# Attention results laid out in DRAM by depth, then head; one load for a block's rows and one for its spread

## The chip, the cores and the metric

The kernel runs on one core of a Trainium2 chip. The metric is the device time of one execution in microseconds (us). The kernel before took 1828.97 us, the median of three runs (1827.23 to 1829.23).

## The reference

It mixes a 32-head attention block and a mixture of 64 tiny experts with a sigmoid gate, over 2048 tokens of width 1024. The change lies in the attention branch: the softmax-weighted sums of the heads, their layout, and the product with `wo`.

```python
B, S, D = x.shape; H = 32; Dh = D // H              # 1, 2048, 1024; Dh = 32
q, k, v = split_heads(x @ wqkv)
p = softmax(einsum("bhqd,bhkd->bhqk", q, k) * Dh ** -0.5)
o = einsum("bhqk,bhkd->bhqd", p, v)
a = o.transpose(0, 2, 1, 3).reshape(B, S, D) @ wo
...
g = sigmoid((x * gate_w).sum(-1, keepdims=True))
return g * a + (1 - g) * b                          # b: the experts' branch
```

## The kernel before

Four stages follow each other. First come the projections of queries and keys and those of the values, which also prepare sums and differences of the blocks of `wo` for a seven-product (Strassen-like) multiplication. Then the attention loop runs over 32 heads of 16 key tiles each (613 to 1644 us). The last 187 us multiply the results by `wo`.

In the attention loop TensorE makes scores into a ring of PSUM banks, ScalarE turns them into exponentials `P`, TensorE multiplies these by the values into `o`. The sums over the keys are formed by VectorE (`acc`) and by GpSimd, which adds four of the 16 tiles of a head (three of the last head's) into a tile `accd` with accumulating DMAs. When a head is done, `finish` copies its unnormalised result to `osb` and stores it to the DRAM tensor `od`. Its sums go to `smd` (`norm_sums`). After each fourth head, `load_r` loads the sums of the four heads of the group as `rr`, and `norm_r` takes the reciprocals, multiplies them by the gate, and stores them to `rd`.

The last stage works on eight blocks of W = 256 tokens. A block n needs two tiles of 128 x 8 x 256 numbers: `OC[n]`, the results of all heads (`load_o`, tile name `V`), and `RB[n]`, the reciprocals, spread over the 32 rows of each head (`load_rb`, tile name `rb` for block 0, else `accd`). Their second index is a group of four heads; there are G = KC = 8 groups. Blocks 0 and 1 go through plain products in fp32r, with high and low parts (`split_hi`, `split_lo`, `split_o`, `wo_mm`); here kc counts the groups, and `z` and `acc` are the high and low part of the results, `woh` and `wol` those of `wo`. The last group of block 0 can only be normalised once the last head's sums have come back from DRAM, so `wo_mm(pa, 0, [KC - 1], ...)` stands last. Blocks 2 to 7 are units of seven products (`unit`): `scale_o` normalises a block in place, `ht.operand` makes the sums S1 to S4 and their parts, and `ht.product` runs a product into one of eight PSUM banks in turn. The other factors of these products come from DRAM by `load_t` (`t0h` to `t3l`).

All orders are written out by hand. Each engine runs its instructions in program order. SyncE (SP in the profile) issues most DMAs, also in order, so a DMA that waits holds up those behind it. Semaphores of eight DMA slots are used in turn, so that a DMA also waits until the eighth before it has landed. Of the tiles `V` and of the tiles `accd` two exist at a time: the load of block n + 2 waits until block n has been used. In the attention loop, `at(step, f, ...)` hangs a call on a key tile.

```python
        if kc == 1:
            norm_sums(H - 1, sm, nc.scalar)
            load_r(G - 1)
...
    for (i, half), ps in pa.items():
        av_mm(0, i, half, ps)
    split_o(0, KC - 1, KC)
    wo_mm(pa, 0, [KC - 1], False, True)
```

Of the kernel before, what the change touches and what calls it, by code (L numbers as in the profile page):

```python
# [9 lines left out]
F32 = mybir.dt.float32  # L10
F32R = mybir.dt.float32r
# [20 lines left out]
def gated_mha_peer_kernel(ctx, tc, xT, wqkv, wv, wo, wq, k12, ug, v, out):  # L32
# [8 lines left out]
    nc = tc.nc  # L41
# [4 lines left out]
    dram = ctx.enter_context(tc.tile_pool(name="dram", bufs=1, space=bass.MemoryType.DRAM))  # L46
# [4 lines left out]
    VD = [dram.tile([S, 512], F32, name=f"vd{i}") for i in range(2)]  # L51
    WPD = dram.tile([128, KC, 512], F32, name="wpd")
    ATD = dram.tile([128, S], F32R, name="atd")
    OD = [dram.tile([128, S], F32, name=f"od{g}") for g in range(G)]
    ZD = dram.tile([1, S], F32, name="zd")
    SMD = [dram.tile([4, S], F32, name=f"smd{g}") for g in range(G)]
    RD = dram.tile([G, 4, S], F32, name="rd")

    TD = [[dram.tile([128, KC // 2, 512], F32R, name=f"t{i}{part}") for part in "hl"] for i in range(4)]
    VPD = [dram.tile([128, D], F32R, name=f"vp{part}") for part in "hl"]  # L60
# [13 lines left out]
    def dma(dst, src, queue=nc.sync):  # L74
        a, b = (ap.bitcast(F32) if ap.dtype == F32R else ap for ap in (dst, src))
        return queue.dma_start(a, b)  # L76
# [16 lines left out]
    def split(hi, lo, src, on=None):  # L93
        nc.scalar.activation(hi, src, AF.Copy)  # L94
        (on or nc.vector).tensor_tensor(out=lo, in0=src, in1=hi.bitcast(F32), op=OP.subtract)
# [805 lines left out]
    zp = Pool("zp", side="right")  # L901
# [210 lines left out]
    early = more[:, KC * W:].rearrange("p (a m) -> p a m", m=512)  # L1112
# [265 lines left out]
    def finish(h):  # L1378
        g, j = divmod(h, 4)
        o = wk.tile([128, 512], F32, name="osb")  # L1380
        nc.scalar.activation(o, O.pop(h), AF.Copy)
        dma(OD[g][32 * j:32 * j + 32, :].rearrange("d (q s) -> q d s", q=NQ), o)


    def norm_sums(h, ps, queue=nc.sync):
# [7 lines left out]
    def load_r(g):  # L1393
        R[g] = wk.tile([128, 128], F32, name="rr", bufs=1)[:, :64]
        dma(R[g], SMD[g].rearrange("j (b m) -> (j b) m", m=64))

    def norm_r(g):
        r = R.pop(g)
        nc.vector.reciprocal(r, r)
        nc.vector.tensor_mul(r, r, G64)  # L1400
        dma(RD[g].rearrange("j (b m) -> (j b) m", m=64), r)


    OC, RB = {}, {}

    def load_o(n, k0, k1, queue=nc.sync):
        if k0 == 0:
            OC[n] = vpool.tile([128, KC, W], F32, name="V")
        for kc in range(k0, k1):
            dma(OC[n][:, kc, :], OD[kc][:, n * W:(n + 1) * W], queue)  # L1410

    def load_rb(n, k0, k1, js=range(4), queue=nc.sync):
        if k0 == 0 and js[0] == 0:
            RB[n] = rb0 if n == 0 else wk.tile([128, KC, W], F32, name="accd")
        for j in js:
            src = RD[k0:k1, j:j + 1, n * W:(n + 1) * W].rearrange("g j s -> j g s")
            dma(RB[n][32 * j:32 * j + 32, k0:k1, :], src.to_broadcast([32, k1 - k0, W]), queue)

    def load_chunk(n, k0, k1, queue=nc.sync):
        load_o(n, k0, k1, queue)  # L1420
# [4 lines left out]
    OH, OL, W0 = {}, {}, []  # L1425
# [38 lines left out]
    at((H - 1) * NT + 13, merge, H - 1)  # L1464
    for k in range(2 * KC):
        c = slice(k % 2 * D // 2, (k % 2 + 1) * D // 2)
        at((8 + k) * NT + 11, dma, raw_wo(k // 2)[:, c], wo[:, k // 2 * D:(k // 2 + 1) * D][:, c])
    for i in range(2):
        at(28 * NT + 6 + i, dma, vhl[:, i], VPD[i])
    at(29 * NT + 13, load_o, 0, 0, 4)  # L1470
    at(30 * NT + 7, load_o, 0, 4, KC - 1)
    at(30 * NT + 13, load_rb, 0, 0, KC - 1, range(2))
    at((H - 1) * NT + 2, load_rb, 0, 0, KC - 1, range(2, 4))
    at((H - 1) * NT + 8, load_rb, 1, 0, KC - 1)
    at((H - 1) * NT + 14, load_rb, 2, 0, KC - 1)
# [113 lines left out]
    def split_o(n, k0, k1):  # L1589
        o = OC[n][:, k0:k1, :]  # L1590
        nc.vector.tensor_mul(o, o, RB[n][:, k0:k1, :])
# [8 lines left out]
    finish(H - 1)  # L1600
    sm = pso.tile([128, 512], F32, name="o")
    list(rowsum(sm, *(P[H - 1, NT - i] for i in (1, 2)), ACC.pop(H - 1)))
    load_o(1, 0, KC - 1, nc.gpsimd)
    split_hi(1)
    for kc in range(1, KC - 1):
        split_hi(kc + 1)
        if kc == 1:
            norm_sums(H - 1, sm, nc.scalar)
            load_r(G - 1)
            for n in range(2):  # L1610
                load_at(n)
# [12 lines left out]
    load_t(2, None, [fin.tile([128, S], F32R, name="t3l")])  # L1624
    load_t(0, *([keep.tile([128, S], F32R, name=f"wo_raw{j}")] for j in range(2)))
# [5 lines left out]
    OH[1] = zp.tile([128, KC, W], F32R, name="z1")  # L1631
    OL[1] = wk.tile([128, KC, W], F32R, name="acc")
# [138 lines left out]
```

## Time and profile before

| what | value |
| --- | --- |
| time, median of three runs | 1828.97 us |
| the profiled execution's own time | 1832.25 us |
| its span, from the first to the last instruction | 1830.4 us |
| mean granted TensorE clock | 0.999 |
| TensorE busy | 1817.8 us (99%) |
| VectorE busy | 1461.4 us (80%) |
| ScalarE busy | 1312.5 us (72%) |
| moved by DMA | 345.24 MB |

All times in rows of the profile are microseconds from the start of the span. A row of the timeline names start, duration, engine, line, operation and tiles; `xN` is the number of merged instructions, and a bracket at its end gives the time for which the engine sat idle before it and what released it. SPq and ACTq are the queues on which SyncE and ScalarE issue DMAs. A row of stages gives the stretch, its length, the busy time and count of each engine (PE is TensorE, PEld its weight loads, DVE VectorE, ACT ScalarE, POOL GpSimd), the granted clock, the busy share of the 16 DMA engines and GB/s. A matmul's row lasts longer than the distance to the next one's start, because matmuls are pipelined.

### The profile page before, as it was taken

The page shows a single profiled execution, that of the slowest core. Times are in us where ns is not written, and L with a number is a line of the kernel's source. Part 1 is how long each engine was busy: PE and PEld are TensorE (multiplying, and loading weights), DVE is VectorE, ACT ScalarE, POOL GpSimd, SP SyncE. Part 2 cuts the span into 40 slices and gives each one's busy share as a digit, 9 for nine tenths or more (in the row PEclk, how much of TensorE's full clock was granted, in tenths as well). Part 3 has the DMA queues.
Part 4 walks back from the last instruction along what each step waited for, and adds up shares of the span by engine and source line. Part 5 has one row for each costly group of instructions (what it writes and reads, how often), then busy time and mean ns, then how long its engine had stood idle before and what let it go on. Part 6 is the DMA issues. An engine that isn't in the chain of part 4 may idle for free.

```text
span 1830.4 us, 26559 instructions
## 1 busy us (share of the span) xinstructions
PE 1817.8 (99%) x10083; PEld 1099.8 (60%) x10083; DVE 1461.4 (80%) x1258; ACT 1312.5 (72%) x1716; POOL 231.7 (13%) x358
## 2 busy tenths in 40 slices
PE   9999999999999999999999999999999999999999
PEld 6777777788888644444444444444444444447787
DVE  7866876789967888888888888888888888884675
ACT  5545544522433699999999999999999999992221
POOL 1222222244001100000000000000000000010000
PEclk9999999999999999999999999999999999999999
DMA  7888689660267777776777777777777777776872
GB/s 271 277 277 280 209 296 286 199 215 9 83 240 247 219 157 178 158 177 154 177 176 164 186 165 182 171 173 167 174 186 159 178 159 182 174 138 180 281 164 78
DMA packets 127441, 345.24 MB, mean 189 GB/s; under 512 B 17168, under 2 KB 57904, under 8 KB 107920
## 3 DMA queue, kind: packets, MB, share of 16 engines
q1 hardware_dynamic: 95688, 193.40, 36.0%
q0 software_dynamic: 28224, 145.92, 34.1%
q10 hardware_dynamic: 3400, 4.20, 1.0%
q8 instruction: 80, 1.31, 0.3%
q14 instruction: 49, 0.40, 0.1%
HBM read 171.76 MB, written 72.36 MB: 133 GB/s over the span
## 4 chain that ended last, share of the span: by engine, by line
PE 88%; DMA 5%; issue 3%; DVE 1%; ACT 1%; SPq 1%; POOL 1%; DVEq 0%; ACTq 0%; POOLq 0%
PE ring L1317 28%; PE o L1338 25%; PE bk L302 15%; PE pa L963 5%; PE bk L724 5%; PE bk L982 2%; PE bk L290 2%; PE bk L341 2%; PE ring L1351 1%; PE bk L963 1%; SPq L76 1%; DMA accd<-rd 1%; DMA accd<-P 1%; DMA smd<-ssb 1%; DMA z<-t2h 1%
## 5 line engine op out<-in xcount | busy, mean ns | idle before, releaser
L1327 ACT ACTIVATE P<-ring 128x1024 f32<-128x1024 f32 (+2 forms) x1031 | 912.7, 983 | 14.5 <-DMA accd<-P 1.9
L1367 DVE TENSOR_TENSOR acc<-acc,P 128x2048 f32<-128x2048 f32 x319 | 730.9, 2291 | 72.6 <-ACT P L1327 47.1
L1338 PE MATMUL o<-P,V 128*32 128x512 f32 x3840 | 464.8, 599 | 0.0
L1317 PE MATMUL ring<-Q,K 98*128 98x512 f32 x1024 | 272.2, 407 | 0.4 <-ACT P L1327 0.3
L1317 PE MATMUL ring<-z,z 98*128 98x512 f32 x1020 | 270.6, 407 | 0.6 <-ACT accd L1327 0.6
L1317 PEld LDWEIGHTS ring<-Q,K 98*128 98x128 f32 x1024 | 182.0, 188 | 144.8 <-ACT P L1327 73.8
L1317 PEld LDWEIGHTS ring<-z,z 98*128 98x128 f32 x1020 | 181.3, 188 | 142.8 <-ACT P L1327 72.0
L1338 PEld LDWEIGHTS o<-P,V 128*32 128x32 f32 x3840 | 98.8, 109 | 223.1 <-issue 214.5
L1360 POOL DMA_DIRECT2D accd<-P x95 | 81.5, 858 | 931.5 <-ACT P L1327 406.5
L1365 DVE TENSOR_TENSOR acc<-P,P 128x2048 f32<-128x2048 f32 x32 | 73.4, 2293 | 74.8 <-ACT P L1327 74.8
L302 PE MATMUL bk<-xh,A 128*128 128x512 f32 x336 | 82.8, 396 | 0.0
L302 PE MATMUL bk<-xh,S 128*128 128x512 f32 x336 | 81.3, 393 | 0.0
L302 PE MATMUL bk<-xl,S 128*128 128x512 f32 x336 | 80.1, 391 | 0.0
L135 ACT ACTIVATE hi<-u 128x512 fp32r<-128x512 f32 x42 | 26.5, 632 | 70.0 <-issue 39.4
L302 PEld LDWEIGHTS bk<-xh,A 128*128 128x128 f32 x336 | 62.1, 188 | 23.8 <-issue 5.0
L1370 DVE TENSOR_TENSOR acc<-acc,accd 128x2048 f32<-128x2048 f32 x32 | 73.1, 2284 | 0.0
L302 PEld LDWEIGHTS bk<-xl,S 128*128 128x128 f32 x336 | 62.8, 188 | 16.3 <-issue 2.5
L302 PEld LDWEIGHTS bk<-xh,S 128*128 128x128 f32 x336 | 62.4, 188 | 14.5 <-issue 1.7
L1327 ACT ACTIVATE accd<-ring 128x1024 f32<-128x1024 f32 (+2 forms) x64 | 62.2, 1032 | 2.3 <-PE ring L1317 2.2
L963 PE MATMUL pa<-woh,acc 128*128 128x512 f32 x192 | 62.2, 389 | 0.0
L511 DVE TENSOR_TENSOR u<-u,bk 128x512 f32<-128x512 f32 x70 | 46.6, 682 | 10.0 <-DMA wpd<-u 5.8
L94 ACT ACTIVATE acc<-V 128x512 fp32r<-128x512 f32 x24 | 14.5, 625 | 50.8 <-DVE V L1576 14.4
(302 smaller groups left out, 2204.9 us busy)
## 6 DMA issues: line engine op xcount, KB each, us to landing
accd<-P POOLq DMA_DIRECT2D x95, 1024.0 KB, 7.6
wqt<-in_wq SPq DMA_DIRECT2D x64, 512.0 KB
wraw<-in_wqkv SPq DMA_DIRECT2D x28, 512.0 KB
kdh<-hi POOLq DMA_DIRECT2D x32, 256.0 KB, 5.3
kdl<-lo POOLq DMA_DIRECT2D x32, 256.0 KB, 6.5
qdh<-hi POOLq DMA_DIRECT2D x32, 256.0 KB, 5.9
qdl<-lo POOLq DMA_DIRECT2D x32, 256.0 KB, 5.9
z<-kdh SPq DMA_DIRECT2D x32, 256.0 KB
```

The source lines that it names most:

```text
L290: nc.tensor.matmul(b0[w, n], AW[PLAIN[w, ki]][a][:, k, :], X[f"B{ki + 1}{n + 1}"][b][:, k, :], start=first, stop=last)
L302: nc.tensor.matmul(ps, a[i][:, k, :], b[j][:, k, :], start=(k == 0 and i == j == 0), stop=(k == HC - 1 and i == 1))
L511: nc.vector.tensor_tensor(out=out, in0=a, in1=b, op=OP.add)
L724: nc.tensor.matmul(ps, x_part(a, t // 4, kc)[:, tok], b, start=first, stop=last)
L963: nc.tensor.matmul(ps, self.a[a][i][:, k, :], self.b[b][j][k], start=(not first and k == 0 and i == j == 0), stop=(k == HC - 1 and i == 1))
L1317: on_ring(nc.tensor.matmul(ring[:, i, :], K[:98, kt * 128:(kt + 1) * 128], Q[:98, qc * 512:(qc + 1) * 512], start=True, stop=True), i)
L1327: on_ring(nc.scalar.activation(P[h, kt][:, q0 * 512:(q0 + m) * 512].rearrange("p (a m) -> p a m", a=m), ring[:, i:i + m, :], AF.Exp, scale ...
L1338: nc.tensor.matmul(O[h][32 * qc:32 * qc + 32, :], Vt[g][:, kt, 32 * j:32 * j + 32], p[:, qc * 512:(qc + 1) * 512], start=(kt == 0), stop=( ...
L1360: nc.gpsimd.dma_start(ACCD[h], P[h, kt], accum_op=OP.add)
L1365: nc.vector.tensor_add(ACC[h], P[h, 0], P[h, kt])
L1367: nc.vector.tensor_add(ACC[h], ACC[h], P[h, kt])
L1370: nc.vector.tensor_add(ACC[h], ACC[h], ACCD[h])
```

## The change

The eight tensors `od0` to `od7` become one, ordered by quarter of the tokens, depth, head in its group, half, group and token. Row p of a block's tile is then 4 * depth + head instead of 32 * head + depth, and the 8 x 256 numbers of a row lie together in DRAM. `rd` is laid out likewise by head, block and group. So `load_o` becomes one DMA with up to 8 KB in a piece where it was one for each group with pieces of 1 KB, and `load_rb` becomes one DMA where it was four. The stores of `finish` now come in pieces of 1 KB where they were 2 KB. The rows of `wo` are loaded in the new order of rows. TensorE's instructions and their order stay the same. Several loads and steps move.

```diff
-    OD = [dram.tile([128, S], F32, name=f"od{g}") for g in range(G)]
+    OD = dram.tile([NQ, 32, 4, 2, KC, W], F32, name="od")
+    wo_rows = wo.rearrange("(j d) m -> d j m", j=4)
...
-    RD = dram.tile([G, 4, S], F32, name="rd")
+    RD = dram.tile([4, S // W, KC, W], F32, name="rd")
...
-            dma(early[:, j], wo[:, c0:c0 + 512])
+            dma(early[:, j], wo_rows[:, :, c0:c0 + 512])
...
-        dma(OD[g][32 * j:32 * j + 32, :].rearrange("d (q s) -> q d s", q=NQ), o)
+        dma(OD[:, :, j, :, g, :].rearrange("q d n s -> (q d) n s"),
+            o.rearrange("p (n s) -> p n s", n=2))
...
-        dma(RD[g].rearrange("j (b m) -> (j b) m", m=64), r)
+        dma(RD[:, :, g, :].rearrange("j n (q m) -> (j n) q m", m=64), r)
...
-        for kc in range(k0, k1):
-            dma(OC[n][:, kc, :], OD[kc][:, n * W:(n + 1) * W], queue)
+        dma(OC[n][:, k0:k1, :], OD[n // 2, :, :, n % 2, k0:k1, :].rearrange("d j g s -> (d j) g s"), queue)
...
-        for j in js:
-            src = RD[k0:k1, j:j + 1, n * W:(n + 1) * W].rearrange("g j s -> j g s")
-            dma(RB[n][32 * j:32 * j + 32, k0:k1, :], src.to_broadcast([32, k1 - k0, W]), queue)
+        src = RD[:, n, k0:k1, :].rearrange("j g s -> j (g s)")[None]
+        dma(RB[n][:, k0:k1, :].rearrange("p g s -> p (g s)"),
+            src.to_broadcast([32, 4, (k1 - k0) * W]), queue)
...
-    at(30 * NT + 13, load_rb, 0, 0, KC - 1, range(2))
-    at((H - 1) * NT + 2, load_rb, 0, 0, KC - 1, range(2, 4))
+    at(30 * NT + 13, load_rb, 0, 0, KC - 1)
     at((H - 1) * NT + 8, load_rb, 1, 0, KC - 1)
-    at((H - 1) * NT + 14, load_rb, 2, 0, KC - 1)
...
-    load_o(1, 0, KC - 1, nc.gpsimd)
     split_hi(1)
     for kc in range(1, KC - 1):
         split_hi(kc + 1)
...
                 load_at(n)
+            load_o(1, 0, KC - 1)
             pso.close()
         split_lo(kc)
         wo_mm(pa, 0, [kc], False, False)
-    norm_r(G - 1)
+        if kc == HC:
+            norm_r(G - 1)
     for n in range(2):
         load_chunk(n, KC - 1, KC)
-    load_rb(2, KC - 1, KC)
+    load_rb(2, 0, KC)
...
+    split_o(1, 0, HC)
+    split_o(0, KC - 1, KC)
+    load_o(2, 0, KC)
     load_t(0, *([keep.tile([128, S], F32R, name=f"wo_raw{j}")] for j in range(2)))
...
-    split_o(0, KC - 1, KC)
     wo_mm(pa, 0, [KC - 1], False, True)
-    for k0, k1 in ((0, HC), (HC, KC)):
-        split_o(1, k0, k1)
-    load_o(2, 0, KC)
+    split_o(1, HC, KC)
     load_at(2)
     load_t(2, [zp.tile([128, S], F32R, name="z0")], None)
     load_t(1, *([keep.tile([128, S], F32R, name=f"wo_raw{2 + j}")] for j in range(2)))
+    load_rb(3, 0, KC)
+    load_o(3, 0, KC)
     pa1 = banks4()
...
-    load_rb(3, 0, KC, queue=nc.scalar)
-    load_o(3, 0, KC)
```

The first place is SyncE's queue at the end of the attention loop. Before, from the loads of the reciprocals of blocks 1 and 2 (two tiles `accd`) to the loads of the last group (`od7`; the first `V` is block 0's, the other block 1's):

```order
L76 DMA accd_12321<-rd_88 32x7x256 x4
L76 DMA accd_12402<-rd_88 32x7x256 x4
L76 DMA od7_78<-osb_12457 4x32x512
L76 DMA rr_12490<-smd7_87 128x64
L76 DMA at_12492<-atd_70 128x256
L76 DMA at_12494<-atd_70 128x256
L76 DMA rd_88<-rr_12490 128x64
L76 DMA V_11936<-od7_78 128x256
```

The same place now:

```order
L77 DMA accd_12306<-rd_81 128x1x1792
L77 DMA od_71<-osb_12434 128x2x256
L77 DMA rr_12459<-smd7_80 128x64
L77 DMA at_12461<-atd_70 128x256
L77 DMA at_12463<-atd_70 128x256
L77 DMA V_12465<-od_71 128x1792
L77 DMA rd_81<-rr_12459 32x4x64
L77 DMA V_11929<-od_71 128x256
```

One DMA stands where eight stood ahead of the last head's store. Block 2's reciprocals are gone from here. Block 1's results (`V_12465`), which GpSimd issued in seven DMAs before, stand between the load of the sums and the store of the reciprocals.

The second place is VectorE in block 0, where the last group's sums are turned into reciprocals. Before, from group 4's parts (`wol4`) to those of block 1:

```order
L1553 TENSOR_TENSOR wol4_12435<-wo_raw1_5501,woh4_12428 128x1024
L1556 TENSOR_TENSOR acc_12286<-V_11936,z0_12285 128x256
L1549 TENSOR_TENSOR V_11936<-V_11936,rb0_5505 128x256
L1553 TENSOR_TENSOR wol5_12436<-wo_raw2_5502,woh5_12429 128x1024
L1556 TENSOR_TENSOR acc_12286<-V_11936,z0_12285 128x256
L1553 TENSOR_TENSOR wol6_12437<-wo_raw2_5502,woh6_12430 128x1024
L1556 TENSOR_TENSOR acc_12286<-V_11936,z0_12285 128x256
L1399 RECIPROCAL rr_12490<-rr_12490 128x64
L1400 TENSOR_TENSOR rr_12490<-rr_12490,G64_102 128x64
L1553 TENSOR_TENSOR wol7_12438<-wo_raw3_5503,woh7_12431 128x1024
L95 TENSOR_TENSOR wol0_12440<-wo_raw3_5503,woh0_12439 128x1024
L1591 TENSOR_TENSOR V_11936<-V_11936,rb0_5505 128x256
```

The same place now; block 1's tile is `V_12465`, block 0's `V_11929`:

```order
L1552 TENSOR_TENSOR wol4_12412<-wo_raw1_5494,woh4_12405 128x1024
L1555 TENSOR_TENSOR acc_12271<-V_11929,z0_12270 128x256
L1401 RECIPROCAL rr_12459<-rr_12459 128x64
L1402 TENSOR_TENSOR rr_12459<-rr_12459,G64_95 128x64
L1548 TENSOR_TENSOR V_11929<-V_11929,rb0_5498 128x256
L1552 TENSOR_TENSOR wol5_12413<-wo_raw2_5495,woh5_12406 128x1024
L1555 TENSOR_TENSOR acc_12271<-V_11929,z0_12270 128x256
L1552 TENSOR_TENSOR wol6_12414<-wo_raw2_5495,woh6_12407 128x1024
L1555 TENSOR_TENSOR acc_12271<-V_11929,z0_12270 128x256
L1552 TENSOR_TENSOR wol7_12415<-wo_raw3_5496,woh7_12408 128x1024
L96 TENSOR_TENSOR wol0_12417<-wo_raw3_5496,woh0_12416 128x1024
L1590 TENSOR_TENSOR V_12465<-V_12465,accd_12306 128x1024
```

The reciprocal moved ahead of five operations on groups 5 and 6, and the first half of block 1 moved ahead of the last group of block 0.

The third place is SyncE's queue behind that. Before, from the last of the eight DMAs for block 2's results (`V_12654`) to the loads of `t3h` into `woh`, behind which block 3's results stood (its reciprocals were on ScalarE's queue):

```order
L76 DMA V_12654<-od7_78 128x256
L76 DMA at_12663<-atd_70 128x256
L76 DMA z0_12665<-t2h_93 128x2048
L76 DMA wo_raw2_12667<-t1h_91 128x2048
L76 DMA wo_raw3_12668<-t1l_92 128x2048
L76 DMA out_0<-rb0_5505 128x512 x4
L76 DMA woh0_12439<-t3h_95 128x512
```

The same place now, from block 2's reciprocals (`accd_12572`) on:

```order
L77 DMA accd_12572<-rd_81 128x1x2048
L77 DMA t3l_12577<-t2l_87 128x2048
L77 DMA V_12587<-od_71 128x2048
L77 DMA wo_raw0_12589<-t0h_82 128x2048
L77 DMA wo_raw1_12590<-t0l_83 128x2048
L77 DMA at_12619<-atd_70 128x256
L77 DMA z0_12621<-t2h_86 128x2048
L77 DMA wo_raw2_12623<-t1h_84 128x2048
L77 DMA wo_raw3_12624<-t1l_85 128x2048
L77 DMA accd_12627<-rd_81 128x1x2048
L77 DMA V_12629<-od_71 128x2048
L77 DMA out_0<-rb0_5498 128x512 x4
```

Block 2's results (`V_12587`) stand ahead of `t0h` instead of behind `t0l`, and block 3's loads (`accd_12627`, `V_12629`) ahead of the stores of block 0.

More of the change, by code (lines that the diff above doesn't have):

```diff
@@ L1408, in load_o, with load_rb @@
             OC[n] = vpool.tile([128, KC, W], F32, name="V")
-        for kc in range(k0, k1):
-            dma(OC[n][:, kc, :], OD[kc][:, n * W:(n + 1) * W], queue)
-    def load_rb(n, k0, k1, js=range(4), queue=nc.sync):
-        if k0 == 0 and js[0] == 0:
+        dma(OC[n][:, k0:k1, :], OD[n // 2, :, :, n % 2, k0:k1, :].rearrange("d j g s -> (d j) g s"), queue)
+    def load_rb(n, k0, k1, queue=nc.sync):
+        if k0 == 0:
             RB[n] = rb0 if n == 0 else wk.tile([128, KC, W], F32, name="accd")
-        for j in js:
-            src = RD[k0:k1, j:j + 1, n * W:(n + 1) * W].rearrange("g j s -> j g s")
-            dma(RB[n][32 * j:32 * j + 32, k0:k1, :], src.to_broadcast([32, k1 - k0, W]), queue)
+        src = RD[:, n, k0:k1, :].rearrange("j g s -> j (g s)")[None]
+        dma(RB[n][:, k0:k1, :].rearrange("p g s -> p (g s)"),
+            src.to_broadcast([32, 4, (k1 - k0) * W]), queue)
     def load_chunk(n, k0, k1, queue=nc.sync):
@@ L1466, in gated_mha_peer_kernel @@
         c = slice(k % 2 * D // 2, (k % 2 + 1) * D // 2)
-        at((8 + k) * NT + 11, dma, raw_wo(k // 2)[:, c], wo[:, k // 2 * D:(k // 2 + 1) * D][:, c])
+        at((8 + k) * NT + 11, dma, raw_wo(k // 2)[:, c], wo_rows[:, :, k // 2 * D:(k // 2 + 1) * D][:, :, c])
     for i in range(2):
@@ L1624, in gated_mha_peer_kernel @@
     load_t(2, None, [fin.tile([128, S], F32R, name="t3l")])
+    OH[1] = zp.tile([128, KC, W], F32R, name="z1")
+    OL[1] = wk.tile([128, KC, W], F32R, name="acc")
+    split_o(1, 0, HC)
+    split_o(0, KC - 1, KC)
+    load_o(2, 0, KC)
     load_t(0, *([keep.tile([128, S], F32R, name=f"wo_raw{j}")] for j in range(2)))
@@ L1628, in gated_mha_peer_kernel @@
         av_mm(0, i, half, ps)
-    split_o(0, KC - 1, KC)
     wo_mm(pa, 0, [KC - 1], False, True)
-    OH[1] = zp.tile([128, KC, W], F32R, name="z1")
-    OL[1] = wk.tile([128, KC, W], F32R, name="acc")
-    for k0, k1 in ((0, HC), (HC, KC)):
-        split_o(1, k0, k1)
-    load_o(2, 0, KC)
+    split_o(1, HC, KC)
     load_at(2)
```

## The prediction

> **What bounds the kernel now.** The page's first part comes first.
>
> ```profile
> PE 1817.8 (99%) x10083; PEld 1099.8 (60%) x10083; DVE 1461.4 (80%) x1258; ACT 1312.5 (72%) x1716; POOL 231.7 (13%) x358
> L1327 ACT ACTIVATE P<-ring 128x1024 f32<-128x1024 f32 (+2 forms) x1031 | 912.7, 983 | 14.5 <-DMA accd<-P 1.9
> ```
>
> TensorE is the bound and leaves only 12.6 us. The second row shows the attention loop's exponentials, which run almost without a gap: the change touches neither these nor TensorE's work. What it can win lies in the last stage. There TensorE's timeline has three stalls, and the chain of waits gives the pace without one:
>
> ```profile
> 1661.38 1.07 PE L1522 MATMUL pa<-wol,z 128*128 128x512 f32 x4
> 1665.91 1.97 PE L1529 MATMUL pa<-vhl,at 128*128 128x512 f32 x8
> 1669.27 0.96 PE L1522 MATMUL pa<-woh,z 128*128 128x512 f32 x3 [1.39 <-ACT z L94]
> ...
> 1698.21 0.39 PE L963 MATMUL pa<-woh,acc 128*128 128x512 f32 x1
> 1699.36 0.47 PE L963 MATMUL pa<-z,s 128*128 128x512 f32 x1 [0.76 <-ACT osb L1678]
> ...
> 1720.08 0.39 PE L963 MATMUL pa<-woh,acc 128*128 128x512 f32 x1
> 1722.73 0.67 PE L963 MATMUL pa<-z,s 128*128 128x512 f32 x1 [2.26 <-DVE rb L969]
> 1727.15 1.08 PE L963 MATMUL pa<-wo_raw,s 128*128 128x512 f32 x4
> ...
> 1740.03 13.60 PE pa L963 x60
> 1760.88 13.60 PE pa L963 x60
> ```
>
> 60 matmuls in 13.60 us are 0.227 for one. By starts, the stalls cost: 1669.27 - 1665.91 - 8 x 0.227 = 1.55 us; 1699.36 - 1698.21 - 0.227 = 0.92; 1722.73 - 1720.08 - 0.227 = 2.42. Behind the third, a product's 12 matmuls took 1727.15 - 1722.73 = 4.42 us instead of 2.72: 1.70 more, at a clock of 0.60 (third number from the right in these rows of stages):
>
> ```profile
> 1722.80:1727.10 4.30, 4.30 (x12) 3.43 (x13) 3.52 (x7) 1.15 (x2) 0.00 (x0) 0.60 0.73 87
> 1750.00:1826.20 76.20, 76.16 (x336) 62.74 (x335) 49.53 (x75) 14.73 (x25) 0.00 (x0) 1.00 0.48 129
> ```
>
> From 1750 us on TensorE never waits. All there is to win in this stage is 1.55 + 0.92 + 2.42 + 1.70 = 6.59 us.
>
> **First stall: the last group's reciprocals.** The chain of waits and the timeline:
>
> ```profile
> 1650.21 10.26 DMA smd<-ssb
> 1660.54 0.34 SPq L76 DMA_DIRECT2D rr<-smd  x1
> 1662.86 0.55 DVE L1399 RECIPROCAL rr<-rr 128x64 f32<-128x64 f32 x1 [3.67 <-DMA rr<-smd]
> 1663.70 0.32 SPq L76 DMA_DIRECT2D rd<-rr  x1
> 1665.18 1.72 SPq L76 DMA_DIRECT2D rb<-rd  x4
> 1668.34 0.43 DVE L1591 TENSOR_TENSOR V<-V,rb 128x256 f32<-128x256 f32 x1 [2.40 <-DMA rb<-rd]
> 1668.80 0.42 ACT L94 ACTIVATE z<-V 128x256 fp32r<-128x256 f32 x1 [10.20 <-DVE V L1591]
> ...
> 1631.86 15.13 SPq L76 DMA_DIRECT2D accd<-rd  x8
> 1647.10 1.83 SPq L76 DMA_DIRECT2D od<-osb  x1
> V<-od POOLq DMA_DIRECT2D x7, 128.0 KB, 11.5
> 1650.00:1658.00 8.00, 8.00 (x37) 6.59 (x36) 6.46 (x12) 6.72 (x11) 0.00 (x0) 1.00 0.67 172
> ```
>
> The tiny store of the sums takes 10.26 us while the store `rd` took 1665.18 - 1663.70 = 1.48. In flight beside it are block 1's `V` from GpSimd (seven times 128 KB, landing 11.5 us after issue), block 2's `accd`, issued last of the eight, and the store `od`; the DMA engines are 0.67 busy. The change takes block 2's `accd` out, moves `V` behind the sums, and lets `od` go when its copy is done. So I price the sums like `rd`: issue 1.06 us on ScalarE's queue, then 1.16 (1.48 less its 0.32 of issue), plus 2.32 for loading `rr`: it lands at 1650.21 + 1.06 + 1.16 + 2.32 = 1654.8 us. The other end is 1662.9, as now.
>
> The added wait is the reciprocal's on VectorE, now ahead of groups 5 and 6:
>
> ```profile
> 1655.83 0.42 DVE L1549 TENSOR_TENSOR V<-V,rb 128x256 f32<-128x256 f32 x1
> 1656.17 1.22 DVE L1553 TENSOR_TENSOR wol<-wo_raw,woh 128x1024 fp32r<-128x1024 f32 x1
> 1658.78 0.42 DVE L1556 TENSOR_TENSOR acc<-V,z 128x256 fp32r<-128x256 f32 x1
> 1669.59 1.22 DVE L1591 TENSOR_TENSOR V<-V,accd 128x1024 f32<-128x1024 f32 x1
> 1670.85 1.06 ACT L94 ACTIVATE z<-V 128x1024 fp32r<-128x1024 f32 x1 [1.63 <-DVE V L1591]
> ```
>
> VectorE reaches it at 1655.8, after the sums land, so it waits for nothing. From there, with 1.22 for the low part of half a block too: 0.84 (1662.86 to the issue of `rd` at 1663.70), 3.37 (1655.83 to 1659.20), two `wol` 2.44, half of block 1 now ahead of the last group 1.22 + 1.06 + 1.22, then 0.46 + 0.47 until TensorE has `z`: 11.1 us, 1666.9. TensorE wants it at 1665.91 + 8 x 0.227 = 1667.7. The stall of 1.55 goes, with 0.8 to spare; sums that land after 1656.6 bring it back.
>
> Block 1's load, 0.9 MB, stands ahead of the store `rd`: 917 KB at the 422 GB/s shown below is 2.2 us, done by about 1657, when `rd` is issued. Hidden by groups 5 and 6.
>
> **Second and third stall: loads in SyncE's queue.**
>
> ```profile
> 1672.59 15.92 SPq L76 DMA_DIRECT2D V<-od  x8
> 1689.23 9.99 DMA z<-t2h
> 1707.50 4.78 SPq L76 DMA_DIRECT2D V<-od  x8
> 1713.45 1.23 DVE L1576 TENSOR_TENSOR V<-V,accd 128x1024 f32<-128x1024 f32 x1 [3.99 <-DMA V<-od]
> ...
> 1632.00:1636.00 4.00, 4.00 (x27) 1.95 (x25) 3.90 (x3) 4.00 (x5) 0.00 (x0) 1.00 1.12 219
> 1674.00:1678.00 4.00, 4.00 (x19) 3.34 (x18) 2.72 (x4) 2.03 (x3) 0.00 (x0) 1.00 1.01 422
> ```
>
> Eight DMAs for block 2 held SyncE for 15.92 us, so `t2h` was issued at 1689.23 and landed at 1699.22: that, not ScalarE, ended the second stall. Now one DMA loads block 2's results instead of eight, and pieces of 8 KB move at 422 GB/s (the `t0` loads) where those of 1 KB move at 219. Block 2's load waits for VectorE's last use of block 0, about 1667.5. Behind it follow `t0h`, `t0l` and `t2h`, four times 1.05 MB: 10 us, landing near 1680, 17 us before it is wanted. 0.92 us gone.
>
> In the third stall VectorE waited 3.99 us for block 3's results, issued at 1707.50, and so released the product's bank late. The new place needs block 1's tiles free (about 1671); with what stands ahead it is the last of 8.5 MB from 1667.5 on: 20 us, landing near 1688, while VectorE asks at 1709.5. Freed of 3.99 us, it releases the bank 1.6 us before TensorE wants it. 2.42 us and, with the clock drop, 1.70 go. The next to be late would be `t3h`, issued behind block 0's stores near 1690 and wanted in unit 2's last product, over 20 us later.
>
> [...]
>
> **The loop.** Block 0's reciprocals come in one load in head 30:
>
> ```profile
> 1598.41 1.03 SPq L76 DMA_DIRECT2D rb<-rd  x2
> 1599.79 10.48 DMA accd<-P
> 1610.35 1.94 ACT L1327 ACTIVATE P<-ring 128x512 f32<-128x512 f32 x2 [0.93 <-DMA accd<-P]
> 1611.00 0.50 PE L1317 MATMUL ring<-Q,K 98*128 98x512 f32 x1 [0.31 <-ACT P L1327]
> ```
>
> The slow accumulation (10.48 us) starts amid these loads of 458 KB into 64 rows. Now 917 KB go in large pieces. Ends: ScalarE's 0.93 won, or as much lost again; I take TensorE's 0.31 as won, the loads being the shorter at 422 GB/s. Stores of `od` in 1 KB pieces have 32 us each; the loads of `wo` have the same sizes: nothing.
>
> **The sum.** 6.59 + 0.31 = 6.90 us. The profiled execution took 1832.25 us (span 1830.4), 3.28 above the median; it would take 1825.35. The median, 1828.97, becomes 1822.1.
>
> **Rivals.** 0.2%, 3.7 us, is about what can be told from no change.
>
> - The first stall stays (sums land at 1657 to 1659, or block 1 ahead of the last group costs more): 1822.1 + 1.55 = 1823.6. The mere 0.8 us to spare speak for it. 0.14.
> - The slow stretch stays, its cause another than the wait: 1822.1 + 1.70 = 1823.8. Against it: in the 76 us without a stall the clock is 1.00. [...] 0.04.
> - The sums land at 1662.9 as now. VectorE is held 7.0 us; `wol` of group 5 comes at 1662.9 + 0.84 + 0.34 + 1.22 = 1665.3 where TensorE wants it at 1661.4: 3.9, then 2.4 for the last group, and 1.7 of slow clock. 8.0 - 1.55 = 6.45 lost against 5.35 won: 1830.1, no change. 0.12.
> - The third stall isn't the load's but ScalarE's and VectorE's own pace: won 1.55 + 0.92 + 0.31 only, 1826.2. Against it: units 4 to 7 run without a stall. 0.07.
> - Slower: spreading 8 KB from one place to 32 rows is slow. Place: `accd` of blocks 4 to 7. TensorE's unit lasts 20.9 us (1740.03 to 1760.88 in the chain), its DMAs 0.48 of it, 10 us, of which 1 MB at 219 GB/s, 4.8, is this load. It decides once the load takes over 15.7 us, below 67 GB/s. At a quarter of 219 it takes 19.2: 3.5 late in each of four units, 14 less 6.9: 1836.1. Against it: the same numbers are spread 32 times now. 0.13.
>
> **Chances and range.** The forecast has 0.50. Faster: 0.50 + 0.14 + 0.04 = 0.68; same: 0.12 + 0.07 = 0.19; slower 0.13. The range runs from 1820.4 (0.6 more from the loop, 1.1 of spread between runs) to 1830.6 (late sums and 0.5 of spread), leaving out the slow spread and little else.
>
> **What would show it.** `rr` on VectorE starting before 1657 us counted from a loop that ends at 1643.8; no wait of TensorE over 0.3 us between 1644 and 1826; clock 1.00 there; no wait for `V<-od` on VectorE in units 2 and 3. A reciprocal that waits, a slow stretch without a wait, or `accd<-rd` ending waits in units 3 to 6 would prove the rivals.

## The result, and the profile after

The changed kernel takes 1825.84 us, the median of 11 executions (1824.19 to 1826.57). The kernel before takes 1829.84 us, the median of 11 on the same chip (1827.23 to 1833.42). The ratio is 0.9977, with an interval of 0.9967 to 0.9986: some 4.2 us are won, between 2.6 and 6.0. The forecast was 6.9, more than that interval holds. The profiled execution of the changed kernel took 1824.19 us, with a span of 1822.4.

Its first part of the page, TensorE's and ScalarE's share above all:

```profile
PE 1814.7 (100%) x10083; PEld 1099.5 (60%) x10083; DVE 1461.8 (80%) x1258; ACT 1312.8 (72%) x1716; POOL 227.5 (12%) x351
```

TensorE's timeline at the places of the three stalls, and the rows of stages for the place of the slow stretch and for the tail (the last three numbers are the granted clock, the DMA share and GB/s):

```profile
1665.02 1.98 PE L1528 MATMUL pa<-vhl,at 128*128 128x512 f32 x8
1666.84 1.07 PE L1521 MATMUL pa<-woh,z 128*128 128x512 f32 x4
...
1695.62 0.39 PE L964 MATMUL pa<-woh,acc 128*128 128x512 f32 x1
1695.85 0.39 PE L964 MATMUL pa<-z,s 128*128 128x512 f32 x1
...
1716.47 0.39 PE L964 MATMUL pa<-woh,acc 128*128 128x512 f32 x1
1716.70 0.39 PE L964 MATMUL pa<-z,s 128*128 128x512 f32 x1
...
1717.50:1721.80 4.30, 4.30 (x21) 3.56 (x20) 4.30 (x6) 0.71 (x2) 0.00 (x0) 1.00 0.72 229
1750.00:1815.00 65.00, 65.00 (x288) 53.84 (x287) 38.88 (x57) 11.98 (x20) 0.00 (x0) 1.00 0.24 91
```

No bracket is left. 1666.84 - 1665.02 is 8 matmuls of 0.227 us; the other two pairs lie one matmul apart. The clock is 1.00 where it was 0.60.

The sums of the last group and the loads that followed late, from the queues, VectorE and ScalarE:

```profile
1649.32 1.06 ACTq L77 DMA_DIRECT2D smd<-ssb  x1
1651.08 0.34 SPq L77 DMA_DIRECT2D rr<-smd  x1
1654.88 0.55 DVE L1401 RECIPROCAL rr<-rr 128x64 f32<-128x64 f32 x1
1655.72 0.59 SPq L77 DMA_DIRECT2D rd<-rr  x1
1659.07 0.54 SPq L77 DMA_DIRECT2D rb<-rd  x1
1664.65 0.42 DVE L1590 TENSOR_TENSOR V<-V,rb 128x256 f32<-128x256 f32 x1
1665.10 0.42 ACT L95 ACTIVATE z<-V 128x256 fp32r<-128x256 f32 x1 [1.63 <-DVE V L1590]
...
1666.00 0.33 SPq L77 DMA_DIRECT2D V<-od  x1
1668.84 0.32 SPq L77 DMA_DIRECT2D z<-t2h  x1
1673.12 0.32 SPq L77 DMA_DIRECT2D V<-od  x1
...
1673.15 2.36 DVE L1575 TENSOR_TENSOR V<-V,accd 128x1024 f32<-128x1024 f32 x2 [2.49 <-DMA V<-od]
1701.60 2.36 DVE L1575 TENSOR_TENSOR V<-V,accd 128x1024 f32<-128x1024 f32 x2
```

The store of the sums landed at most 1.76 us after its issue, when `rr` was issued (10.26 before); the reciprocal waits for nothing, and `z` is ready at 1665.52, 1.3 us before TensorE wants it. `t2h` is issued at 1668.84 instead of 1689.23, block 3's results at 1673.12 instead of 1707.50; VectorE takes them at 1701.60 without a wait. One sign that the prediction asked for is missing: VectorE still waits 2.49 us for block 2's results, but TensorE doesn't wait for that.

The DMA engines in two stretches, before and then after:

```profile
1665.00:1695.00 30.00, 28.61 (x126) 23.37 (x125) 10.69 (x13) 4.14 (x6) 0.00 (x0) 1.00 0.81 207
1695.00:1720.00 25.00, 24.24 (x107) 19.77 (x107) 12.78 (x19) 6.61 (x12) 0.00 (x0) 1.00 0.98 365
```

```profile
1665.00:1695.00 30.00, 30.00 (x134) 24.84 (x133) 10.80 (x15) 4.98 (x8) 0.00 (x0) 1.00 1.02 421
1695.00:1720.00 25.00, 25.00 (x112) 20.72 (x111) 18.91 (x28) 7.94 (x14) 0.00 (x0) 1.00 0.58 220
```

From 1665 to 1695 us 421 GB/s are moved instead of 207, so that the engines have time to spare behind 1695. Two loads, of `od` and of `rd`, and the order changed at once; the experiments take them apart.

The copies of the sums of heads 30 and 31 measure the loop, before and then after:

```profile
1597.24 0.60 ACT L1388 ACTIVATE ssb<-ring 128x512 f32<-128x512 f32 x1 [0.38 <-PE ring L1351]
1630.48 0.60 ACT L1388 ACTIVATE ssb<-ring 128x512 f32<-128x512 f32 x1
```

```profile
1597.17 0.60 ACT L1390 ACTIVATE ssb<-ring 128x512 f32<-128x512 f32 x1 [0.38 <-PE ring L1352]
1629.59 0.60 ACT L1390 ACTIVATE ssb<-ring 128x512 f32<-128x512 f32 x1
```

33.24 us became 32.42. From the loop's end (1643.79 and 1642.89) to the end of the span it is 186.6 us before and 179.5 after, 7.1 less. The spans of the two profiled executions differ by 8.0 us, the medians by 4.0. That was the first question.

### The profile page after: what moved, and what is told of

It reads as the page before. It is cut to its first block, busy times and chain, and to the rows that moved or that the text cites. A ratio compares the mean times of both kernels' runs of the same rounds, so it can differ in the third digit from the quotient of the medians.

```text
span 1822.4 us, 26410 instructions
## 1 busy us (share of the span) xinstructions
PE 1814.7 (100%) x10083; PEld 1099.5 (60%) x10083; DVE 1461.8 (80%) x1258; ACT 1312.8 (72%) x1716; POOL 227.5 (12%) x351
## 4 chain that ended last, share of the span: by engine, by line
PE 94%; issue 2%; DVE 2%; DMA 1%; ACT 0%; POOL 0%; ACTq 0%; SPq 0%; DVEq 0%; POOLq 0%
PE ring L1318 29%; PE o L1339 26%; PE bk L303 15%; PE pa L964 6%; PE bk L725 5%; PE pa L1521 2%; PE bk L983 2%; PE bk L291 2%; PE bk L964 2%; PE bk L342 2%; PE ring L1352 1%; PE pa L1528 1%; DVE xh L970 1%; DMA t1l<-xl 0%; PE bk L191 0%
```

## The experiments

"Behind the loop" is the time from the loop's end to the end of the span, 186.6 and 179.5 above. Each run was compared with the kernel before on its own chip.

### Does the loss stand in every execution? (two kernels, unchanged)

> The kernel before, unchanged, profiled a second time. The medians of before and after lie 4.0 us apart, the two profiled executions 8.0 us. Theory A (the four losses are the same in every execution; the profiled execution was long for another reason): the second profile shows the stalls again at 1.55, 0.92 and 2.42 us and the slow stretch at 1.70, each within 0.3 us, and the rest of the difference lies in the attention loop. Theory B (the losses hang on when DMAs land and vary from run to run): at least one of the four is missing or changed by over 1 us, and the sum, 6.6 us in the first profile, goes with the execution's own time. The ratio to before is 1.000 by both, within 0.001.

Measured: 1832.08 us (12 executions, 1828.92 to 1834.63), ratio 1.0006 (0.9997 to 1.0015). The profiled execution took 1828.92 us, the shortest of them. TensorE's timeline and a row of stages at its one stall:

```profile
1721.00 0.47 PE L963 MATMUL pa<-z,s 128*128 128x512 f32 x1 [1.89 <-DVE rb L969]
...
1722.00:1726.00 4.00, 4.00 (x19) 3.30 (x18) 3.22 (x7) 1.15 (x2) 0.00 (x0) 1.00 0.63 83
```

The first stall is gone, the second is 0.21 us by starts, the third 1.89 us of idle time, and no slow stretch follows. Behind the loop it is 182.3 us, 4.3 less than in the first profile. The spans differ by 3.3, as its loop ended 1.0 later. So theory B holds: the losses vary from execution to execution, and here they sum to 182.3 - 179.5 = 2.8 us, not 7.1. The clock of the other executions agrees: of 18 of the kernel before beside this run the eight longest (1831.69 us and more) show a mean clock of 0.999, the four shortest 1.000.

> The changed kernel, unchanged, profiled a second time. Its first profile was of the fastest of its 11 runs (1824.19 us, median 1825.84) and had no wait of TensorE over 0.6 us behind the loop. Theory A (the changed order has no loss left behind the loop): again no stall between 1644 us and the end, clock 1.00, the stretch from the loop's end to the last instruction 179.5 us within 0.3, and an execution that takes longer has it in the attention loop or before. Theory B (a stall comes back in some executions, since z is ready only 1.3 us ahead of TensorE): the last stage is 180.5 us or longer in a slower execution, with a wait for z or a slow stretch in it. Ratio to before 0.9977 within 0.0015.

Measured: 1826.16 us, ratio 0.9969 (0.9958 to 0.9981): on this chip 3.5 to 7.7 us are won. The profiled execution took 1826.34 us. Behind the loop it has 179.5 us again, with no stall and clock 1.00; the 2.1 us more lie ahead of the loop's end (1645.01). Theory A holds for the changed kernel: its last stage is the same in both.

### The layouts alone, the order alone

```diff
-    load_rb(2, 0, KC)                    # and the other moved lines, back at their old places
+    at((H - 1) * NT + 14, load_rb, 2, 0, KC - 1)
...
+    load_o(1, 0, KC - 1, nc.gpsimd)
...
+    load_rb(3, 0, KC, queue=nc.scalar)   # behind plain_out(0, pa) and load_t(3, ...)
+    load_o(3, 0, KC)
```

> The new layouts of od and rd, and so one DMA for each load, but every load and step at its old place (block 1's results on GpSimd's queue ahead of the sums, block 2's reciprocals ahead of the last head's store, the last group's reciprocals behind groups 5 and 6, block 3's loads behind block 0's stores and t3). Theory of the prediction (stalls 1 and 2 come from piecewise loads in the queues): SyncE is no longer held for 15.92 us by block 2's results, t2h lands by about 1685 and the stall of 0.92 goes; the sums still share the DMA engines with 2.7 MB of loads, but these move at about 400 GB/s and not 219, so the sums land between 1656 and 1659 and the first stall is 0 to 1 us; block 3's results are issued near 1707 as before but take about 3 us and not 6 to land, VectorE waits about 1 us and not 3.99, so the third stall (2.42) and the slow stretch (1.70) mostly go: 5 to 6.5 us won in its profile, nearly all that the whole change wins, and a ratio within 0.001 of the changed kernel's. Rival (the places matter, not the pieces): the third stall and the slow stretch stay, 1 to 2.5 us won, and about 4 us are left to the order.

Measured: 1825.34 us, ratio 0.9968 (0.9956 to 0.9981), 179.5 us behind the loop, no stall, 32.4 us between the two copies of sums. Its row of stages, and SyncE's issue of block 3's results:

```profile
1665.00:1695.00 30.00, 30.00 (x134) 24.85 (x133) 13.53 (x17) 5.93 (x9) 0.00 (x0) 1.00 0.96 363
...
1695.67 0.32 SPq L77 DMA_DIRECT2D V<-od  x1
```

The layouts win all of it; the new order adds nothing that can be measured. The store of the sums, issued at 1651.57 us, had landed by 1654.51 although `accd` and `V` were still in flight beside it, so the first stall needed no reordering either.

> The old layouts with one DMA for each group and each head, but every load and step at its new place. Theory of the prediction: block 3's results are loaded well ahead, so the third stall (2.42) and the slow stretch (1.70) go; but block 1's seven DMAs of 1 KB pieces stand on SyncE between the load of the sums and the store of the reciprocals, 917 KB at 219 GB/s, 4.2 us, and more where one waits for the eighth before it, so rb of the last group lands 4 to 8 us later than in the changed kernel, and TensorE waits 3 to 6 us for z where it waited 1.55: between 3 us won and 3 us lost against before. Rival (the places matter, not the pieces): as fast as the changed kernel, 4 us ahead of before, and z on time.

Measured: 1846.39 us, ratio 1.0083 (1.0071 to 1.0096): slower by 15 us, further than the theory's 3. ScalarE in the loop, SyncE, VectorE and TensorE in unit 2:

```profile
1615.36 3.77 ACT L1327 ACTIVATE P<-ring 128x512 f32<-128x512 f32 x4 [6.14 <-DMA accd<-P]
...
1700.05 18.87 SPq L76 DMA_DIRECT2D V<-od  x8
1719.01 1.90 SPq L76 DMA_DIRECT2D out<-rb  x4
1721.90 0.69 DVE L1584 COPY rb<-pa 128x512 f32<-128x512 f32 x1 [15.50 <-DMA out<-rb]
1722.65 1.22 PE L1527 MATMUL pa<-vhl,at 128*128 128x512 f32 x2 [9.96 <-DVE rb L1584]
```

The theory's place was wrong: the sums made no stall. What cost was the four spreads of block 0 at once in head 30, which delayed an accumulation (6.14 us of ScalarE's time), and block 3's eight loads in their new early place: SyncE stood 18.87 us in them, the stores of block 0 waited behind, and TensorE stood 9.96 us for a bank. With old loads the new order is harmful.

### Which load? One DMA for `od`, then each layout by itself

```diff
-        for kc in range(k0, k1):
-            dma(OC[n][:, kc, :], OD[kc][:, n * W:(n + 1) * W], queue)
+        dma(OC[n][:, k0:k1, :], OD[k0:k1, :, n * W:(n + 1) * W].rearrange("g p s -> p g s"), queue)
```

> The kernel before with od as one tensor in its old order of rows and columns, so that a block's results come in one DMA of 1 KB pieces instead of eight DMAs; nothing else differs. Theory A (the number of DMAs: eight of them hold SyncE's queue for 15.92 us, and t2h, t3h and block 3's results follow late): SyncE is held under 2 us by block 2's results, block 3's results are issued 8 to 12 us earlier, stalls 2 and 3 and the slow stretch go, and the stretch from the loop's end to the end of the span falls from 182.3 to 186.6 us to 180.5 or less; ratio to before 0.997 to 0.998. Theory B (the size of the pieces: 1 KB moves at 219 GB/s where 8 KB moves at 422): the one DMA takes as long to land as the eight, what follows is as late, the stretch stays at 182 to 187 us and the ratio is within 0.001 of 1.

Measured: 1830.57 us, ratio 1.0004 (0.9994 to 1.0014), 183.3 us behind the loop. SyncE's issue of block 2's results, and VectorE's use of them:

```profile
1671.86 0.60 SPq L76 DMA_DIRECT2D V<-od  x1
...
1695.91 2.36 DVE L1575 TENSOR_TENSOR V<-V,accd 128x1024 f32<-128x1024 f32 x2 [17.77 <-DMA V<-od]
```

SyncE is free after 0.60 us, and the results are there only 24 us later; TensorE waits 1.70 us ahead of unit 2 instead. Theory B holds: it isn't the hold on SyncE.

```diff
-    OD = [dram.tile([128, S], F32, name=f"od{g}") for g in range(G)]
+    OD = dram.tile([NQ, 32, 4, 2, KC, W], F32, name="od")
...
-            dma(RB[n][32 * j:32 * j + 32, k0:k1, :], src.to_broadcast([32, k1 - k0, W]), queue)
+            dst = RB[n].rearrange("(d j) g s -> j d g s", j=4)[j]
+            dma(dst[:, k0:k1, :], src.to_broadcast([32, k1 - k0, W]), queue)
```

> The new layout of od alone, with its one load of 8 KB pieces; rd keeps its old layout and four DMAs of 1 KB pieces for each spread, and every step stands at its old place. Theory A (od's loads carry the win of the last stage): no second or third stall and no slow stretch, 179.5 to 181 us behind the loop; the first stall may keep up to 1 us, since eight DMAs for accd still stand ahead of the last head's store; the 0.85 us of the loop (from the copy of one head's sums to that of the next, 33.3 us before and 32.4 after) is not won. Ratio 0.9975 to 0.9985. Theory B (rd's spread loads carry it): 182 to 187 us behind the loop, ratio 0.999 to 1.

The new order of rows goes with `od`'s layout, so each DMA of a spread now writes every fourth row.

Measured: 1831.03 us, ratio 0.9998 (0.9989 to 1.0008), 184.2 us behind the loop. SyncE, VectorE and TensorE around the third stall, a piece of the chain of waits, and SyncE's waits for spreads from 1664 to 1716 us (total, times, longest):

```profile
1704.88 0.49 SPq L77 DMA_DIRECT2D V<-od  x1
1712.60 2.36 DVE L1578 TENSOR_TENSOR V<-V,accd 128x1024 f32<-128x1024 f32 x2 [6.71 <-DMA V<-od]
1721.17 0.47 PE L964 MATMUL pa<-z,s 128*128 128x512 f32 x1 [2.64 <-DVE rb L970]
...
1678.93 22.29 DMA accd<-rd
...
SPq L77 <- DMA accd<-rd: 20.9, 4, 9.0
```

Stalls 1 and 2 are gone, as theory A had it, but the third stays at 2.64 us, with a slow stretch behind it: the ratio shows no gain. SyncE waits 20.9 us for the four DMAs of block 3's spread (`accd<-rd`); the one of the chain is the last of them, issued on ScalarE's queue at 1678.93 and landing 22.29 us later. The loop's part was expected wrongly: it was won here too (32.44 us between the copies).

> The new layout of rd alone, with one DMA for each spread; od keeps its eight tensors and eight DMAs, and every step stands at its old place (block 0's spread in head 30). Theory A (od's loads carry the last stage, rd's the loop): 32.4 us and not 33.3 between the copies of the sums of heads 30 and 31, the sums of the last group up to 2 us earlier, but SyncE still held for about 16 us by block 2's results, so the third stall stays near 2 us: 182 to 186 us behind the loop, ratio 0.999 to 1. Theory B (rd's spread carries the last stage): 180 us behind the loop, ratio 0.997.

```diff
+        src = RD[:, n, k0:k1, :].rearrange("j g s -> j (g s)")[:, None]
+        dma(RB[n][:, k0:k1, :].rearrange("p g s -> p (g s)"),
+            src.to_broadcast([4, 32, (k1 - k0) * W]), queue)
```

Measured: 1857.14 us, ratio 1.0143 (1.0126 to 1.016). In the old order of rows the one DMA is written as 4 heads x 32 rows, and behind the issue of block 0's spread (1599.49 us) the DMA share settles here:

```profile
1608.00:1618.00 10.00, 4.94 (x29) 2.15 (x32) 5.99 (x3) 4.31 (x5) 0.86 (x1) 0.85 0.26 75
```

The DMA engines' mean busy share is 0.26, and the accumulation behind came 5.69 us late for ScalarE. This run says nothing on rd's layout; the next one does, with four DMAs of 32 rows:

```diff
-            src = RD[k0:k1, j:j + 1, n * W:(n + 1) * W].rearrange("g j s -> j g s")
-            dma(RB[n][32 * j:32 * j + 32, k0:k1, :], src.to_broadcast([32, k1 - k0, W]), queue)
+            src = RD[j:j + 1, n, k0:k1, :].rearrange("j g s -> j (g s)")
+            dst = RB[n][32 * j:32 * j + 32, k0:k1, :].rearrange("p g s -> p (g s)")
+            dma(dst, src.to_broadcast([32, (k1 - k0) * W]), queue)
```

> The kernel before with rd in its new layout, and each spread still in four DMAs, one for each head of the group, now with up to 8 KB in a piece; od and every place as before. It replaces the run in which one DMA spread rd over the old order of rows and the DMA engines were busy at 0.25 to 0.26, 66 to 75 GB/s. Theory A (the engines' time is shared by all transfers between 1665 and 1695 us; either layout alone frees only part of it, as od's alone did at 265 GB/s and no gain): no 70 GB/s stretch, 230 to 300 GB/s from 1665 to 1695 us, at least one of the stalls stays, 181 to 184 us behind the loop, ratio 0.998 to 1.0005. Theory B (rd's spread alone carries the last stage): 363 GB/s or more there, no stall, 179.5 to 180 us, ratio 0.997. By both, head 31's sums are copied 33.3 us after head 30's, since the 0.85 us of the loop came with od's layout.

Measured: 1825.62 us, ratio 0.9964 (0.9951 to 0.9976), 179.8 us behind the loop, no stall, 32.42 us between the copies. The row of stages, SyncE, VectorE's wait for block 3, and SyncE's waits for spreads from 1664 to 1716 us:

```profile
1665.00:1695.00 30.00, 30.00 (x134) 24.82 (x133) 13.62 (x17) 5.93 (x9) 0.00 (x0) 1.00 0.85 294
...
1670.46 13.44 SPq L76 DMA_DIRECT2D V<-od  x8
1700.90 4.70 SPq L76 DMA_DIRECT2D V<-od  x8
1706.77 1.23 DVE L1577 TENSOR_TENSOR V<-V,accd 128x1024 f32<-128x1024 f32 x1 [3.03 <-DMA V<-od]
...
SPq L76 <- DMA accd<-rd: 5.0, 1, 5.0
```

Theory A, mine by then, fell: larger pieces in the spreads of `rd` alone win as much as the whole change. Eight DMAs still hold SyncE for 13.44 us, and VectorE still waits 3.03 us for block 3, yet TensorE stands nowhere. SyncE's waits for spreads are 5.0 us where they were 20.9 with `od`'s layout alone and 10.4 in the kernel before. The loop's gain, which both theories denied to this run, came too.

### Number of DMAs, and the third stall by itself

```diff
+        for j in range(4):
+            src = RD[j:j + 1, n, k0:k1, :].rearrange("j g s -> j (g s)")
+            dst = RB[n].rearrange("(d j) g s -> j d (g s)", j=4)[j]
+            dma(dst[:, k0 * W:k1 * W], src.to_broadcast([32, (k1 - k0) * W]), queue)
```

> The changed kernel with each spread in four DMAs again, one for each head of the group (every fourth row), pieces still up to 8 KB. Theory A (the size of the pieces counts, not the number of DMAs): no stall behind the loop, 179.5 us within 0.5, 360 to 420 GB/s from 1665 to 1695 us, ratio to before within 0.001 of the changed kernel's 0.9969. Theory B (SyncE's queue counts): the twenty or so added DMAs delay t2h and block 3's results, and a stall of 0.5 to 2.5 us comes back: 180 to 183 us, ratio 0.998 to 0.9995.

Measured: 1825.83 us, ratio 0.9968 (0.9957 to 0.9979), 179.6 us behind the loop, no stall. Its row of stages:

```profile
1665.00:1695.00 30.00, 30.00 (x134) 24.82 (x134) 11.62 (x16) 4.98 (x8) 0.00 (x0) 1.00 0.94 369
```

Theory A holds: four DMAs for a spread cost nothing.

```diff
     load_o(2, 0, KC)
+    load_o(3, 0, KC, nc.gpsimd)
...
-    load_o(3, 0, KC)
```

> The kernel before with one change: block 3's results are issued by GpSimd, which has nothing to do there, right behind those of block 2 in the program, and no longer by SyncE behind t3. Theory A (the third stall is that load's lateness): VectorE no longer waits 4 us for V<-od ahead of unit 3, the third stall (1.9 and 2.4 us in two profiles) and the slow stretch go; stalls 1 and 2 stay as the execution has them (0.2 to 2.5 us together): 180 to 182.5 us behind the loop, ratio 0.998. Rival (ScalarE's and VectorE's own pace sets the third stall): about 2 us stay there without the wait. Second rival (the load only collides earlier): t2h and t3h land later and TensorE waits for them, ratio 1 or above.

Measured: 1830.73 us, ratio 1.0001 (0.999 to 1.0013); the profiled execution, one of the longer ones at 1834.23 us, has 187.8 us behind the loop. SyncE in block 2's results, and TensorE at the places of the second and third stall:

```profile
1673.36 19.38 SPq L76 DMA_DIRECT2D V<-od  x8
...
1702.94 0.76 PE L963 MATMUL pa<-z,s 128*128 128x512 f32 x1 [3.47 <-DMA z<-t2h]
...
1726.80 0.39 PE L963 MATMUL pa<-z,s 128*128 128x512 f32 x1
```

The second rival is right for this execution: block 2's load takes 19.38 us instead of 15.92, and `t2h` makes TensorE wait 3.47 us instead of 0.76. VectorE no longer waits for block 3's results and the third stall is gone, but that doesn't show that this load was its cause: TensorE came to the third place only at 1726.80, 5.5 us after VectorE had released the bank (1721.28). Over 12 executions nothing was won.

### Which spread? (open)

Two kernels took the one of rd's layout with four DMAs, and wrote block 3's spread, or all but block 3's, without joining the groups of a row (`src = RD[j:j + 1, n, k0:k1, :]`).

> The kernel before with rd in its new layout and four DMAs for each spread, as in the run that won all of it (179.8 us behind the loop, block 3's results issued at 1700.90 us), but block 3's spread alone again in pieces of 1 KB. Theory A (block 3's spread, which stands just ahead of block 3's results, is what makes those late): the third stall is back at 1.5 to 2.6 us, 182 to 184 us behind the loop. Theory B (all the spreads' engine time counts, block 3's is one of four that lie between 1632 and 1700 us): block 3's results are issued 1 to 2 us later, VectorE's wait for them grows from 3 us to 4, and the stall stays under 0.5 us: 179.8 to 180.3 us.

> The reverse of the run beside it: rd in its new layout, four DMAs for each spread, block 3's spread in pieces of up to 8 KB and all the others in pieces of 1 KB. Theory A (block 3's spread alone): no third stall, 180 to 181.5 us behind the loop with what the first two stalls may keep, ratio 0.997 to 0.998. Theory B (all the spreads' engine time): block 3's results are issued near 1704 to 1706 us as before, the third stall stays at 1.5 us or more, 182 us or longer, ratio 0.9985 or above. The 0.85 us of the loop is lost by both if block 0's spread in head 30 made it.

Measured: 1825.39 and 1825.62 us, ratio 0.9972 (0.9961 to 0.9982) both, 179.8 us behind the loop both. The packets of the DMA queues between 1590 and 1760 us, in the kernel before, in that of rd's layout, and in these two:

```profile
DMA packets 20298, 33.01 MB, mean 194 GB/s; under 512 B 2408, under 2 KB 15276, under 8 KB 18840
```

```profile
DMA packets 15977, 35.27 MB, mean 207 GB/s; under 512 B 2556, under 2 KB 9596, under 8 KB 13953
```

```profile
DMA packets 15809, 34.93 MB, mean 205 GB/s; under 512 B 2540, under 2 KB 9580, under 8 KB 13790
```

```profile
DMA packets 15879, 35.00 MB, mean 206 GB/s; under 512 B 2532, under 2 KB 9572, under 8 KB 13875
```

The pieces stayed large in both: 9580 and 9572 packets under 2 KB, where the kernel of rd's layout has 9596 and the kernel before 15276. So these are repeats of the run with rd's layout (its 179.8 us stand three times). Which of the spreads carries the third stall was not tested; SyncE's waits above point to block 3's.

## Why the prediction was right, and where it failed

One line for each kernel: GB/s between 1665 and 1695 us; how long after the loop's end block 3's results are issued; TensorE's idle time in the third stall; the time behind the loop.

| kernel | GB/s | block 3 issued | third stall | behind the loop | ratio |
| --- | --- | --- | --- | --- | --- |
| before, two profiles | 207, 225 | 63.7, 61.2 | 2.26, 1.89 | 186.6, 182.3 | |
| `od` in one DMA | 217 | 61.4 | 0.44 | 183.3 | 1.0004 |
| `od`'s layout | 265 | 60.6 | 2.64 | 184.2 | 0.9998 |
| `rd`'s layout, four DMAs | 294 | 56.0 | 0 | 179.8 | 0.9964 |
| both layouts, old order | 363 | 50.5 | 0 | 179.5 | 0.9968 |
| changed, two profiles | 421, 401 | 30.2, 30.0 | 0 | 179.5, 179.5 | 0.9977, 0.9969 |

- **The stalls and the slow stretch** go as forecast: 7.1 us less behind the loop where the sum of the terms was 6.59.
- **The size failed in one step**: "The profiled execution took 1832.25 us (span 1830.4), 3.28 above the median; it would take 1825.35. The median, 1828.97, becomes 1822.1." That took the 3.28 for something the change doesn't touch. For that execution the forecast is close: 1825.35 against the 1824.19 of the changed kernel's profiled one, and the loop and the last stage, each 0.5 above its terms, make up most of the rest. Luck has a part in that: 1824.19 is the shortest of its 11 executions, and the second profile of the changed kernel took 1826.34. And the second profile of the kernel before shows that the losses are what varies, 7.1 us in one execution and 2.8 in the other. With the loop's 0.8 the change is worth 3.6 us by the one profile and 7.9 by the other; the medians, 4.0 and 5.1 us apart in two comparisons, lie between.
- **The loop** was mis-sized: 0.31 us taken, 0.82 measured. I took TensorE's wait; ScalarE, with 32.03 us of work in the 33.30 from 1597.20 to 1630.50 us of the kernel before, sets the pace, so all but 0.1 of its 0.93 counted. The cause named was the loads of `rd`, and they do it alone; but `od`'s layout alone does it too (32.44 us between the copies), while `od` in one DMA of 1 KB pieces does not (33.24). Which part of that layout does it was not tested.
- **The first stall**: the store of the sums was priced at 1.06 + 1.16 = 2.22 us and took at most 1.76; `rr` was there when VectorE asked at 1654.88, and `z` had 1.3 us to spare instead of 0.8. The rivals on late sums fell. The reasons given, three transfers taken out of the way, weren't needed: with all three still there, in large pieces, the store took at most 2.94 us and the stall was gone.
- **The second and third stall**: that late loads made them agrees with the traces: with `od`'s layout alone the chain of waits runs from the landing of block 3's results (1712.58) over VectorE and ScalarE to TensorE's late start at 1721.17. No run changed that load's time alone without making TensorE late as well. "Eight DMAs for block 2 held SyncE for 15.92 us" was the wrong step: one DMA for eight didn't end the stalls, and with eight DMAs and large spreads they were gone. In the table the third goes with the time at which block 3's results are issued: none at up to 56.0 us after the loop's end (57.4 in one of the two repeats), the full one at 60.6. The 0.44 at 61.4 is small because TensorE itself had stood for 2.33 us ahead of it, in three waits of 0.29, 1.70 and 0.34.
- **What held SyncE** can be read from its waits. A DMA of SyncE also waits for DMAs of ScalarE's queue here: in the kernel before, SyncE issued four of the eight loads in 3.73 us and then waited 8.3 us for a DMA of block 3's spread, in 1 KB pieces on ScalarE's queue. With `od`'s layout alone it waited 20.9 us in turn for the four DMAs of that spread; with `rd`'s layout alone 5.0 us, in the changed kernel 2.0. This fits that `rd`'s pieces are enough, with block 3's results issued 4.6 us earlier than with `od`'s. The prediction had the rates, 219 GB/s against 422, and used them for single transfers; block 3's spread as something that SyncE waits for is in none of its terms. No run changed this spread alone.
- **The order**, credited with the third stall and the spare time of the first, won nothing on top of the layouts.
- **The slow spread**, the rival on the other side, didn't come: no unit waits for `accd`. Its price is real, though: with 4 heads outermost the engines moved 75 GB/s (1608 to 1618 us), near the point of 67 from which it was to decide. No trace of the kernel before shows the quarter of 219 GB/s at which it was priced; the run with 4 heads outermost shows a busy share of 0.26.
- **The slow stretch** goes with its stall (clock 1.00 from 1717.50 to 1721.80 us, 0.60 before), and so its rival fell.

## What to carry to other kernels

When a profiled execution is longer than the median, first find out whether the losses you mean to remove are what makes it longer: a second profile of the same kernel answers that. Where many transfers share a stretch, add up their engine time before blaming the queue that visibly stands: a DMA that holds its queue can be only the one that waits for slow neighbours, as block 2's did here (8.3 of its 15.92 us). Make the pieces large in the layout (`rd`'s alone gave a ratio of 0.9964), and check which dimension of a spread is outermost (75 GB/s with 4 heads outermost).

## What the runs showed of the hardware

**The clock.** In these runs it fell after every stall of 2.26 us or more, and after none of 1.89 us or less: behind 1.89 it stayed at 1.00 (shown above), behind 2.26, in the first profile of the kernel before, a row of stages shows

```profile
1722.80:1726.20 3.40, 3.40 (x9) 2.66 (x10) 2.62 (x5) 1.15 (x2) 0.00 (x0) 0.50 0.73 88
```

with 0.99 in the next 2.80 us, and behind 2.64, 3.47 and 9.96 us it fell as well (0.65 from 1721.20 to 1725.50 us with `od`'s layout, 0.66 from 1700 to 1710 with block 3's load on GpSimd, 0.50 from 1722.60 to 1726.00 with the order alone).

**A spread with 4 heads outermost.** Behind the issue of a spread written as 4 x 32 rows, the mean busy share of the DMA engines was 0.26, at 75 GB/s (1608 to 1618 us); spreads written as 32 x 4 rows are among the transfers that move at 421 GB/s together in the changed kernel (1665 to 1695 us). The new order of rows, 4 * depth + head, lets one DMA have 32 outermost. Why the first is slow was not shown.

**A small store.** The last head's sums landed at most 1.76 us after the issue of their store in the changed kernel, and 10.26 us after it in the kernel before, with 1 KB pieces in flight beside them. With the layouts alone, where large pieces were in flight, it was at most 2.94 us.
